# Another order and other engines for the operations between a convolution and a mix, and other banks for the last projections

## The chip, the cores and the metric

The kernel runs on one core of a Trainium2 chip. The metric is the device time of a run in microseconds; the time of a kernel is the median of its runs. Profiles are of one execution each, and give the span from the first instruction to the last.

## The reference, cut to what matters

```python
# A: 2048 tokens, 640 channels, bf16
h = _layernorm(A_q) * (1 + ca) + sa                # ca, sa, ga, sb, cb, gb from silu(c) @ w_mod
kv = short_conv(A_k, A_shift_k) * A_v              # 4 taps
y = irfft(rfft(kv, 2S) * rfft(ssm_k, 2S))[:S] + kv * ssm_D   # long convolution over the sequence
x = A_q + ga * (h * y)
# B: gated MLP whose gate mixes tokens
h = _layernorm(x) * (1 + cb) + sb
z = gelu(h @ B_w_in)                               # 640 -> 1728
z1 = z[..., :864]
z2 = _layernorm(z[..., 864:])
g = einsum('ts,bsf->btf', B_w_sp, z2) + b_sp       # 2048 x 2048 over tokens
out = x + gb * ((z1 * g) @ B_w_out)                # 864 -> 640
```

## The kernel before, in words

The long convolution is done as matrix products with cosine tables, in five blocks of 128 channels (u = 0 to 4). Its result multiplies gh (the normalised, modulated q) and is added to xt, the residual stream in bf16: these are the residual adds (`res`, L698), with the statistics of the second layernorm behind them (`ln2`, L704).

Then come 16 token tiles of 128, in four groups of four (`z_group`). For one group:

- aggregates of the statistics (`ag2`, L829), 1/sqrt on POOL (`rstd2`, L190 and L191), a small product (`nmr2`, L833);
- the norm of each tile into a tile of the tag Z (`zx`, L843 on ACT, L845 on POOL, L847 on VectorE);
- a transposition: group 0 by TensorE in two halves (`hfl`, L858), groups 1 to 3 by one DMA transpose on SP's queue (`turn`, L889), into another Z tile; the tag Z has three buffers;
- the modulation by cb and sb (`hmod`, L869 and L871, in group 0; `hmod2`, L895 and L897, in the others), five instructions for a group;
- 16 z products of five matmuls each (`zz`; all of TensorE's helpers stand on L245), eight for z2 and eight for z1, each into one bank of the tags pu or pz (two banks each), which GELU on ACT empties (L920);
- for z2 its own layernorm: bn_stats (`stz`, L926), aggregate (`agz`, L930), `rstdz` on POOL, `nmrz` (L935) and the norm in place (`zn`, L941 on ACT, L943 on VectorE). z1 is laid over tables that are no longer read (M2 and G2).

The mix is a product of 2048 x 2048 weights with z2, done in pairs of token tiles p and p + 8 with seven products of eight matmuls in place of eight (a Strassen-like scheme). It needs sums of weights (S, `s_sum`, L988), differences of z2 (T, `t_sum`, L998: T1, T2, T4, and one in place in z2) and seven products per pair (`product`, L1013). VectorE adds the products and multiplies by z1 (c11, partial, c22, last_sum) into u, a DMA transpose turns u into uT (`turn_u`, L1052), and `project` multiplies uT by w_o (L1137), adds xt (L1139) and stores. The w_o rows are multiplied by gb once they are in (`gbm`, L1077). The weights' tiles wT come by DMA transposes (`load_w`, L974), two per pair.

Everything up to and with the first pair of the mix (p = 0) is recorded as numbered operations, and `ORDER` lists in which order they are emitted and on which engine: P is TensorE, A ScalarE (ACT), D VectorE (DVE), G GpSimd (POOL), S SyncE (SP). The order is written out; each engine's queue is its subsequence, in order, and waits by semaphores. `FILLS` are operations of a few matmuls whose results nobody reads (numbers 1032 to 1037). Pairs 1 to 7 and the projections follow as a plain loop.

For reading the order: group 0's norms are 762, 763, 775, 776; group 1's are 840 to 843, its transpose 844 and its modulation 845 to 849; group 2's 906 to 909, 910 and 911 to 915; group 3's 972 to 975, 976 and 977 to 981. The rstdz of the groups are 828, 894, 960, 1026. The first pair's products are 1070, 1072, 1074, 1076, 1077, 1081, 1083; the T differences 1062 to 1069; the S sums of pairs 0 and 1 are 1054 to 1061; gbm is 1046 to 1052; w_o's loads are 1045; wT's loads 1038 to 1043.

Of the kernel before, what the change touches and what calls it, by code (L numbers as in the profile page):

```python
# [12 lines left out]
F32 = mybir.dt.float32  # L13
I32 = mybir.dt.int32

P = 128
# [50 lines left out]
G675 G519 G520 P521 A522 G509 G510 A500 A132 G708 P487 P584 D502 P513 D488 P511 A512 P491 P489 G503 A490 D514 P515  # L67
G504 D492 S678 G668 P505 P679 A516 A506 G493 D494 P495 A585 D633 D680 P681 D682 A496 P719 A720 D636 S586 P683 D684
P715 P721 A722 D716 P685 D686 D687 P717 A718 P587 A588 P723 P726 P725 G711 P724 G666 D688 D689 G714 D727 D728 D730
D729 D759 P735 P749 P589 A590 D758 D731 D732 G692 D690 G760 D761 D691 A762 G763 P1036 P1037 P764 D736 G611 D734 D750  # L70
D772 D733 D771 D766 S756 D767 D768 P765 A769 D751 P742 S757 A770 P814 G773 D774 G776 A775 D637 D712 D752 D737 D738
D741 P816 A817 G667 D739 P778 A782 D696 A783 D694 D835 D740 P784 D695 D836 P777 D779 D780 D781 G669 D837 D693 D834
D743 G702 G838 A815 D839 D840 D843 G841 A785 D610 D641 D643 D744 D745 P818 G697 D701 D699 A819 D698 P787 A788 D789
D786 P826 A827 A842 S844 P812 P794 A795 D796 D704 A813 G644 S1041 P798 S1045 P808 D642 D746 D901 A799 P820 G845 P824
D790 A809 A821 P801 A825 A847 P805 D703 D848 A802 P791 D849 D645 G846 P822 D810 A806 D807 P886 D705 P853 A792 A823
A887 D748 P882 D966 A883 D755 D903 P850 A854 D640 D900 D647 D793 P884 D700 D646 A851 D747 D902 A885 D754 G904 D905
D906 D909 S1040 G908 A907 S910 G913 D753 P864 S1038 A865 D866 D800 P890 A891 D706 D811 P892 A893 P871 A872 S1039 G911
D648 D969 P857 P860 A858 D859 A861 D803 D1048 P874 A875 D876 P880 A881 P878 P867 D968 A868 G912 P888 A889 D804 A879
G914 D915 P916 A917 D1058 P954 A955 P926 A927 D967 G970 P919 D971 D972 S1043 G975 D862 P923 D1051 A924 P937 G973 A920
D974 S976 A938 D863 P944 A945 D1054 D1055 D869 D870 D1050 D873 D1059 D1061 D1057 P958 A959 D925 S1044 P930 A931 D797  # L80
D877 A977 P933 D980 A934 P946 A947 G828 D829 D928 A831 A832 D833 P952 A953 D939 G978 P940 D1046 A941 G981 G979 P948
P999 A949 D932 P982 A1000 D852 D929 D855 D856 G894 A830 A983 D1053 P985 A986 D918 P1006 A1007 D935 P992 A993 D895 A896
D897 D942 D899 D898 P1012 D987 D1056 P989 A990 D994 P996 A997 D1008 D936 P1014 A1015 D943 D1049 D921 D922 P1003 A1013
P1020 D991 A1004 D1063 D1001 P1018 G960 D961 A963 A1021 A1019 D984 D988 D1005 D998 D1002 S1042 D1009 D995 G1026 D1062
P950 A951 P956 D964 D1027 D1028 D962 D965 D1064 A1029 D1030 A1031 D1065 D1066 D1067 P1024 A1025 P1070 A1071 A957 P1016
A1017 P1072 A1073 D1068 D1069 P1077 D1078 P1081 P1074 P1076 D1082 P1083 D1075 D1079 P1010 S1080 D1084 P1022 A1023
D1052 A1011 S1085 D1060 D1047
"""


# [39 lines left out]
def kernel(  # L130
# [80 lines left out]
    with ExitStack() as pctx:  # L211
# [745 lines left out]
        HT = NT // 2  # L957
        wTs, uTs, Ss, part, us, T = {}, {}, {}, {}, [], {}
# [20 lines left out]
        def a_of(p, i, j):  # L979
            return wTs[p + HT * i][:, j * HT:(j + 1) * HT, :]  # L980

        def s_sum(p, k):
            if k == 0:
                Ss[p] = [bwork.tile([P, HT, P], BF16, tag="S%d" % i, bufs=2, name="S%d" % (i + 1)) for i in range(4)]
            S = Ss[p]
            x, y, o = ((a_of(p, 1, 0), a_of(p, 1, 1), ALU.add), (S[0][:], a_of(p, 0, 0), ALU.subtract),
                       (a_of(p, 0, 0), a_of(p, 1, 0), ALU.subtract), (a_of(p, 0, 1), S[1][:], ALU.subtract))[k]
            nc.vector.tensor_tensor(S[k][:], x, y, op=o)  # L988
# [99 lines left out]
        for p in range(2):  # L1088
            for k in range(4):
                late("D", "ssum1" if (p, k) == (1, 0) else "ssum", lambda p=p, k=k: s_sum(p, k), r=[("wT", p), ("wT", p + HT), ("S", (p, {1: 0, 3: 1}.get(k, k)))], w=[("S", (p, k))])  # L1090
        for k in (1, 2, 3, 4):
            for h in range(2):
                lo, hi, name = h, h + 2, "T%d" % k
# [31 lines left out]
    psB = ctx.enter_context(tc.tile_pool(name="psB", bufs=2, space=bass.MemoryType.PSUM, reuse_waits="tile"))  # L1125
# [2 lines left out]
    def bank(b):  # L1128
        return psB.tile([P, 512], F32, tag="mm", bufs=6, name="ps")

    def project(t):
        ot = bwork.tile([P, D], BF16, tag="ot", bufs=3, name="ot")
        last = t == NT - 1
        for i, (lo, hi) in enumerate(((0, HS), (HS, HS + HS // 2), (HS + HS // 2, D)) if last else ((0, HS), (HS, D))):
            ps = psB.tile([P, 512], F32, tag="o", bufs=2, name="po")
            for ft in range(NFT):
                nc.tensor.matmul(ps[:, :hi - lo], lhsT=uTs[t][:fsz[ft], ft, :], rhs=w_o[:fsz[ft], ft, lo:hi],  # L1137
                                 start=(ft == 0), stop=(ft == NFT - 1))
            nc.vector.tensor_tensor(ot[:, lo:hi], ps[:, :hi - lo], xt[:, t, lo:hi], op=ALU.add)  # L1139
            if last:  # L1140
                (nc.scalar if i == 1 else nc.sync).dma_start(out_nat[:, t, lo:hi], ot[:, lo:hi])
        if not last:
            nc.sync.dma_start(out_nat[:, t, :], ot[:])
# [3 lines left out]
    for p in range(1, HT):  # L1147
# [5 lines left out]
        if nxt:  # L1153
            s_sum(p + 1, 0)
            s_sum(p + 1, 1)
# [11 lines left out]
        if nxt:  # L1167
            project(p - 1)
# [6 lines left out]
        if nxt:  # L1175
            project(p - 1 + HT)
            s_sum(p + 1, 3)
    for p in range(HT - 2, HT):
        project(p)
        project(p + HT)  # L1180


# [28 lines left out]
```

## Time and profile before

| | |
|---|---|
| time before, median of 3 runs | 314.79 us (314.57 to 317.16) |
| profiled execution | 315.2 us, its span 313.4 us |
| TensorE (PE) busy | 297.4 us, 2506 matmuls |
| VectorE (DVE) busy | 252.9 us, 513 instructions |
| ScalarE (ACT) busy | 159.9 us, 286 instructions |
| GpSimd (POOL) busy | 122.7 us, 152 instructions |
| granted TensorE clock | 1.00 |

The stretch from about 128 us to 207.6 us holds the four groups and the first pair of the mix, the stretch to 302 us the other seven pairs, and the rest is the last four projections. In a timeline a row gives the start, the time from the first to the last instruction of the row, the engine and line, output and inputs by their tile names (M, X and G stand for tiles that later hold z1 or z2), and in brackets how long the engine was idle before and who ended it.

### The profile page before, as it was taken

To read this page: it belongs to the slowest core of one execution; us is meant where nothing else is said; L and a number is where in the kernel's file an instruction comes from. 1 tells how busy PE (TensorE), PEld (TensorE's weight loads), DVE (VectorE), ACT (ScalarE), POOL (GpSimd) and SP (SyncE) were. 2 spreads that over 40 slices of the span, in tenths; PEclk is the share of its full clock that TensorE was granted. 3 is DMA by queue.
4 is the path that set the end of the run, shared out by engine and by line. 5 is a ranking of instruction groups with operands and counts; after the bars stand their busy time and mean duration, and the time that the engine had idled before them with its cause. 6 is when DMAs were issued, how large, how long until landed. Compare 5 with 4: busy or idle time off the path is not lost.

```text
span 313.4 us, 6409 instructions
## 1 busy us (share of the span) xinstructions
PE 297.4 (95%) x2506; PEld 196.9 (63%) x2506; DVE 252.9 (81%) x513; ACT 159.9 (51%) x286; POOL 122.7 (39%) x152
## 2 busy tenths in 40 slices
PE   7988999979999998999899999899999999999996
PEld 2665688857889998654454454455565656555554
DVE  7898998979999998989776898987676858567473
ACT  6988799968888957465655775320101010010100
POOL 2532877838988998675435524000000000000000
PEclk9999999999999999999999999999999999999999
DMA  8999899996997769206987700035958385540413
GB/s 163 216 229 239 225 315 250 216 183 165 246 198 145 164 126 323 81 0 138 225 168 156 111 2 1 1 74 120 200 78 192 66 171 118 119 100 4 99 38 104
DMA packets 127953, 45.22 MB, mean 144 GB/s; under 512 B 117071, under 2 KB 127156, under 8 KB 127924
## 3 DMA queue, kind: packets, MB, share of 16 engines
q1 hardware_dynamic: 127770, 44.78, 66.1%
q8 instruction: 19, 0.31, 0.4%
q14 instruction: 10, 0.08, 0.1%
q10 hardware_dynamic: 154, 0.05, 0.1%
HBM read 16.11 MB, written 5.24 MB: 68 GB/s over the span
## 4 chain that ended last, share of the span: by engine, by line
PE 38%; DVE 10%; POOL 5%; DMA 2%; ACT 1%; issue 1%; POOLq 0%; DVEq 0%; ACTq 0%
PE ps L1013 22%; PE po L1137 9%; DVE stz L926 3%; PE pu L245 3%; PE pz L1013 2%; DMA Z<-Z 2%; PE pz L245 2%; DVE S L988 1%; POOL rstdz L191 1%; POOL Z L897 1%; PE pu L1013 1%; DVE st L704 1%; POOL Z L845 1%; ACT X L941 1%; POOL rstd L191 1%
## 5 line engine op out<-in xcount | busy, mean ns | idle before, releaser
L245 PEld LDWEIGHTS <-Z 128*128 128x128 bf16 x320 | 30.7, 98 | 31.2 <-POOL Z L897 4.3
L245 PE MATMUL pu<-X,M 128*128 128x128 bf16 (+1 forms) x480 | 45.8, 237 | 2.2 <-DVE Tf L462 1.9
L245 PEld LDWEIGHTS <-M 128*128 128x128 bf16 x480 | 37.4, 98 | 8.6 <-issue 3.1
L1019 ACT COPY m<-ps 128x432 f32<-128x432 f32 x7 | 3.6, 519 | 72.3 <-PE ps L1013 72.3
L1013 PEld LDWEIGHTS <-S 128*128 128x128 bf16 x256 | 25.0, 98 | 23.6 <-issue 2.0
L476 POOL TENSOR_TENSOR W<-Tf 128x256 bf16<-128x256 f32 x47 | 34.7, 760 | 10.8 <-DVE Tf L462 7.5
L245 PE MATMUL pu<-big,Z 128*128 128x432 bf16 x160 | 33.1, 346 | 1.7 <-ACT X L920 1.3
L245 PE MATMUL pz<-big,Z 128*128 128x432 bf16 x160 | 33.5, 346 | 0.8 <-POOL Z L897 0.8
L248 ACT CAST X<-s 128x1024 bf16<-128x1024 f32 x31 | 31.9, 1028 | 2.9 <-PE s L245 2.7
L1137 PE MATMUL po<-w_o,uT 128*128 128x320 bf16 (+2 forms) x231 | 33.0, 295 | 0.4 <-DVE ot L1139 0.3
L462 DVE TENSOR_TENSOR Tf<-pu,KH 128x1024 f32<-128x1024 f32 x25 | 30.3, 1218 | 2.4 <-PE pu L245 1.3
L1137 PEld LDWEIGHTS <-uT 128*128 128x128 bf16 (+1 forms) x231 | 22.2, 98 | 10.3 <-issue 0.7
L1013 PEld LDWEIGHTS <-wT 128*128 128x128 bf16 x192 | 18.7, 98 | 15.2
L245 PEld LDWEIGHTS <-G 128*128 128x128 bf16 x330 | 24.7, 98 | 2.1 <-issue 0.2
L248 ACT CAST KH<-pu 128x512 bf16<-128x512 f32 x40 | 23.0, 600 | 5.1 <-PE pu L245 5.1
L248 ACT CAST Z<-pz 128x512 bf16<-128x512 f32 x38 | 22.3, 601 | 5.3 <-PE pz L245 5.1
L1013 PE MATMUL ps<-X,wT 128*128 128x432 bf16 x112 | 22.7, 346 | 0.0
L1013 PE MATMUL ps<-T,S 128*128 128x432 bf16 x112 | 22.7, 346 | 0.0
L245 PEld LDWEIGHTS <-X 128*128 128x128 bf16 x288 | 17.7, 97 | 7.7 <-DMA X<-kv_scr 2.4
L1013 PE MATMUL ps<-X,S 128*128 128x432 bf16 x112 | 21.6, 346 | 0.0
L245 PE MATMUL s<-F1bd,X 128*128 128x256 bf16 x128 | 19.2, 272 | 2.0 <-DVE X L400 1.6
L245 PE MATMUL sm<-big,dg 128*128 128x512 bf16 (+1 forms) x80 | 20.4, 379 | 0.0
(181 smaller groups left out, 546.6 us busy)
## 6 DMA issues: line engine op xcount, KB each, us to landing
wm<-in_w_mod_dram SPq DMA_DIRECT2D x6, 800.0 KB, 6.2
xt<-in_A_q_dram SPq DMA_DIRECT2D x4, 640.0 KB, 6.4
out_dram<-ot SPq DMA_DIRECT2D x15, 160.0 KB, 2.1
big<-in_B_w_in_dram SPq DMA_DIRECT2D x2, 1080.0 KB, 9.4
X<-in_A_ssm_k_dram SPq DMA_DIRECT2D x4, 512.0 KB, 5.3
kv_scr<-big SPq DMA_DIRECT2D x4, 512.0 KB, 4.1
X<-kv_scr SPq DMA_DIRECT2D x4, 512.0 KB, 4.9
w_o<-in_B_w_out_dram SPq DMA_DIRECT2D x6, 160.0 KB, 3.1
```

What stands on the lines that cost most here:

```text
L191: nc.gpsimd.tensor_tensor(dst, dst, mhalf[:, 0:dst.shape[1]], op=ALU.pow)
L245: nc.tensor.matmul(o, lhsT=w, rhs=x, start=start, stop=stop)
L248: (e.copy if e is nc.scalar else e.tensor_copy)(dst, src)
L462: e.tensor_tensor(T_[:], (tl[pu] if src is None else tl[src])[:, :, :, None, :].to_broadcast(shape), tl[KH][:, :, None, :, :].to_broadcast ...
L476: e.tensor_tensor(tl[W][:, :, o, :], T_[:, :, 0, o, :], T_[:, :, 1, 1 - o, :], op=ALU.add if o else ALU.subtract)
L704: op("D", "ln2", lambda e, n=n: e.bn_stats(out=st2[:, n, (0, 0, 0, 1, 2)[u], :], in_=xt[:, n, us[0] * DU:(u + 1) * DU]), r=[("xt", (v, n)) ...
L845: e.tensor_scalar(dst, xt[:, n, :], rstd2[:, n:n + 1], nmr2[:, n:n + 1], op0=ALU.mult, op1=ALU.add)
L897: e.tensor_scalar(h, h, cb1_col[:, dt:dt + 1], sb_col[:, dt:dt + 1], op0=ALU.mult, op1=ALU.add)
L926: op("D", "stz", lambda e, i=i, n=n, fc=fc: e.bn_stats(out=stz[:, n, fc, :], in_=tl[z2][:, i, fc * FC:(fc + 1) * FC]), r=[(z2, (i, fc))], ...
L1013: nc.tensor.matmul(ps[:, :FC], lhsT=lhs[:, s_, :], rhs=rhs(s_), start=(s_ == 0 and not more), stop=(s_ == HT - 1), skip_group_check=more)
L1019: nc.scalar.copy(part[p, m][:], part[p, BANK[m]][:, :FC])
L1137: nc.tensor.matmul(ps[:, :hi - lo], lhsT=uTs[t][:fsz[ft], ft, :], rhs=w_o[:fsz[ft], ft, lo:hi], start=(ft == 0), stop=(ft == NFT - 1))
```

## The change: what it does

The last 18 rows of `ORDER` are replaced, `s_sum` allocates its four tiles at whichever of its calls comes first, and the last four calls of `project` take their banks from the tag mm (six banks, used by the mix's products until then) and not from o (two banks). All operations, their shapes and their number stay.

```diff
-D729 D759 P735 P749 P589 A590 D758 D731 D732 G692 D690 G760 D761 D691 A762 G763 P1036 P1037 P764 D736 G611 D734 D750
+D729 D759 G702 D729 P735 P749 G667 D758 D731 P1037 P589 A590 D732 D734 D691 D772 G760 D761 D762 D763 P764 D750 P765 D766
...
         def s_sum(p, k):
-            if k == 0:
+            if p not in Ss:
                 Ss[p] = [bwork.tile([P, HT, P], BF16, tag="S%d" % i, bufs=2, name="S%d" % (i + 1)) for i in range(4)]
...
-    def project(t):
+    def project(t, tag="o"):
...
-            ps = psB.tile([P, 512], F32, tag="o", bufs=2, name="po")
+            ps = psB.tile([P, 512], F32, tag=tag, bufs={"o": 2, "mm": 6}[tag], name="po")
...
     for p in range(HT - 2, HT):
-        project(p)
-        project(p + HT)
+        project(p, "mm")
+        project(p + HT, "mm")
```

The queues that the two orders give, by operation number, from the norms of group 0 on; first TensorE's:

```
before 589 1036 1037 764 765 742 814 816 778 784 777 818 787 826 812 794 798 808 820 824 801 805 791 822
       886 853 882 850 884 864 890 892 871 857 860 874 880 878 867 888
       916 954 926 919 923 937 944 958 930 933 946 952 940 948
       999 982 985 1006 992 1012 989 996 1014 1003 1020 1018 950 956 1024 1070 1016
       1072 1077 1081 1074 1076 1083 1010 1022
after  1037 589 764 765 742 784 816 812 794 777 778 787 818 824 820 814 805 791 822 808 801 826 798
       850 860 864 884 892 867 857 890 880 888 878 871 874 886 853 882
       926 916 948 952 923 946 919 954 933 940 958 930 944 937
       999 982 992 1020 989 985 1006 996 1003 1024 1014 956 1016 1012 950
       1072 1070 1077 1081 1074 1076 1083 1010 1018 1022 1036
```

SP's:

```
before 844 1041 1045 1040 910 1038 1039 1043 976 1044 1042 1080 1085
after  844 1045 1041 1040 910 1038 1044 1039 976 1042 1043 1080 1085
```

POOL's:

```
before 711 666 714 692 760 763 611 773 776 667 669 702 838 841 697 644 845 846 904 908 913 911 912 914
       970 975 973 828 978 981 979 894 960 1026
after  711 666 714 702 667 760 692 773 775 838 841 644 610 669 846 904 908 911 970 973 975 974 828 980
       894 978 981 960 1026
```

Norms, modulations and norms of z2 that change their engine:

| operations | before | after |
|---|---|---|
| 762, 763 (norms, group 0) | ACT, POOL | VectorE |
| 775, 776 | ACT, POOL | POOL, ACT |
| 842 (norm, group 1) | ACT | VectorE |
| 845, 847 (modulation, group 1) | POOL, ACT | VectorE |
| 848, 849 | VectorE | VectorE, ACT |
| 907 (norm, group 2) | ACT | VectorE |
| 912, 913, 914 (modulation, group 2) | POOL | ACT, ACT, VectorE |
| 972, 974 (norms, group 3) | VectorE | ACT, POOL |
| 979, 980 (modulation, group 3) | POOL, VectorE | ACT, POOL |
| 611, 697, 610 (residual adds) | POOL, POOL, VectorE | VectorE, VectorE, POOL |
| zn on VectorE | 9 of 16 | 12 of 16 |

The fill of four (1036) stands before the flips of group 0 (764) in the old order and after the last z product of the recorded part (1022) in the new one. The S sums of pair 1 stand partly behind the first pair's products in the old order (1060) and all before them in the new one; gbm the other way round (six of seven behind them).

More of the change, by code (lines that the diff above doesn't have):

```diff
@@ L69 @@
 P715 P721 A722 D716 P685 D686 D687 P717 A718 P587 A588 P723 P726 P725 G711 P724 G666 D688 D689 G714 D727 D728 D730
-D729 D759 P735 P749 P589 A590 D758 D731 D732 G692 D690 G760 D761 D691 A762 G763 P1036 P1037 P764 D736 G611 D734 D750
-D772 D733 D771 D766 S756 D767 D768 P765 A769 D751 P742 S757 A770 P814 G773 D774 G776 A775 D637 D712 D752 D737 D738
-D741 P816 A817 G667 D739 P778 A782 D696 A783 D694 D835 D740 P784 D695 D836 P777 D779 D780 D781 G669 D837 D693 D834
-D743 G702 G838 A815 D839 D840 D843 G841 A785 D610 D641 D643 D744 D745 P818 G697 D701 D699 A819 D698 P787 A788 D789
@@ L74 @@
[L74 to L87, printed above, removed]
+D759 G702 D729 P735 P749 G667 D758 D731 P1037 P589 A590 D732 D734 D691 D772 G760 D761 D762 D763 P764 D750 P765 D766
@@ new lines @@
+D767 D768 D733 D690 D771 P742 S756 G692 D696 D736 D737 D739 D740 A769 A770 S757 P784 A785 G773 D774 P816 A817 A776
+P812 D637 D695 D836 G775 A813 P794 A795 D693 D741 D738 D834 D837 D694 D835 P777 D779 D780 D781 P778 A782 G838 D839
+D840 D843 A783 P787 A788 D842 G841 D751 S844 D754 D697 D712 D743 D611 D700 D744 D748 G644 P818 P824 A825 D701 A819
+D699 D746 P820 A821 P814 P805 A806 G610 D641 P791 D642 G669 D643 S1045 A815 D796 S1041 P822 A792 A823 D640 D747 D902
+D848 D845 D847 P808 A809 D901 G846 P801 A849 A802 D745 D698 D706 D900 P826 D648 P798 A799 P850 D903 A851 D852 P860
@@ new lines @@
+A827 A861 P864 A865 P884 A885 P892 D1050 G904 D905 P867 A868 D906 D907 D909 A893 P857 P890 A858 A891 S1040 P880 A881
+D793 P888 A889 G908 D803 S910 D755 P878 A879 P871 D645 G911 A913 A872 S1038 P874 P886 D866 D800 A875 P853 P882 A912
+A887 A854 D705 A883 D869 D647 D968 D752 D704 D810 D753 D646 D967 D969 D703 D966 D1060 D914 D1058 G970 D971 D915 A972
+G973 D859 D804 P926 P916 A917 D1059 G975 D807 A927 D811 D789 P948 D876 S1044 D1053 P952 S1039 D1056 D928 D873 D877
+A949 P923 A924 G974 D870 P946 A947 A953 D855 P919 A920 D786 D790 D925 D797 P954 D1054 A955 D862 D863 G828 P933 A934
@@ new lines @@
+S976 G980 P940 A979 A941 P958 A977 P930 A931 D856 G894 D1061 A959 D929 D1055 D1057 D942 D935 P944 A945 P937 D918 A938
+D895 D898 A899 D897 D896 G978 D921 D922 D829 D832 G981 D939 D943 P999 D932 D936 G960 P982 A1000 D830 A983 D984 S1042
+D1001 P992 A993 P1020 A1021 D961 P989 A990 D1063 D833 P985 A986 P1006 A1007 A962 P996 A997 D965 P1003 A1004 D831 P1024
+D994 D991 D995 D987 D988 P1014 D1008 P956 D1005 D1009 A1025 A1015 P1016 D998 D1002 G1026 D963 D1062 A964 D1064 D1027
+D1030 A957 A1017 P1012 A1013 S1043 P950 A1029 A951 P1072 A1073 D1028 P1070 D1031 D1065 A1071 D1066 D1067 P1077 P1081
@@ L88 @@
+D1068 D1069 D1078 D1082 P1074 P1076 P1083 D1075 D1079 S1080 P1010 A1011 D1084 D1048 P1018 A1019 P1022 A1023 D1049
+D1052 S1085 D1051 P1036 D1047 D1046
 """
```

## The prediction

> **What bounds the kernel now.** I read the busy shares first, then the waits of TensorE, then its timeline at each wait, and last a table of stages.
>
> ```profile
> PE 297.4 (95%) x2506; PEld 196.9 (63%) x2506; DVE 252.9 (81%) x513; ACT 159.9 (51%) x286; POOL 122.7 (39%) x152
> ```
>
> TensorE is the bound and the change gives it no matmul more or fewer, so the time can only move by what TensorE waits. Its waits from 150 us on (us in total, times, longest), then its timeline around them (start, us, idle before in brackets):
>
> ```profile
> PE pz L1013 <- ACT G L920: 1.8, 1, 1.8
> PE pu L245 <- ACT X L920: 1.3, 1, 1.3
> PE pz L245 <- POOL Z L897: 0.8, 1, 0.8
> PE pu L245 <- POOL Z L897: 0.4, 2, 0.2
> PE po L1137 <- DVE ot L1139: 0.3, 1, 0.3
> ```
>
> ```profile
> 128.87 1.89 PE L245 MATMUL s<-ident 128*128 128x512 bf16 x7
> ...
> 132.37 1.36 PE L245 MATMUL pz<-big,Z 128*128 128x432 bf16 x5
> ...
> 147.41 1.08 PE L245 MATMUL pz<-big,Z 128*128 128x432 bf16 x5
> 149.79 1.17 PE L245 MATMUL pu<-big,Z 128*128 128x432 bf16 x5 [1.30 <-ACT X L920]
> ...
> 178.12 0.53 PE L245 MATMUL pz<-big,Z 128*128 128x432 bf16 x2
> 179.40 0.72 PE L245 MATMUL pz<-big,Z 128*128 128x432 bf16 x3 [0.75 <-POOL Z L897]
> 179.96 1.08 PE L245 MATMUL pu<-big,Z 128*128 128x432 bf16 x5
> ...
> 194.20 1.08 PE L245 MATMUL pz<-big,Z 128*128 128x432 bf16 x5
> 197.02 1.62 PE L1013 MATMUL pz<-T,S 128*128 128x432 bf16 x8 [1.75 <-ACT G L920]
> ```
>
> The reader is to see that each wait is one late hand-over at the head of a token group, and that the fills at 128.87 stand in a wait too. From 207.80 the mix has none:
>
> ```profile
> 207.80:302.06 94.26, 94.26 (x560) 54.61 (x559) 63.90 (x113) 8.94 (x16) 0.00 (x0) 1.00 0.53 111
> ```
>
> So whatever reaches the mix's second pair earlier ends earlier by as much. A z product (five matmuls) lasts 0.913 (150.79 to 151.70), a mix product 1.46 (197.02 to 198.48).
>
> [...] the trace keeps clock 1.00 over the 1.75 us wait, so moving fills away should cost no clock. [...] an S sum (L988) took 1.08 at 169.11 beside GpSimd's norms, 0.67 alone. This is the unknown in every VectorE sum below.
>
> **The change part by part.** I walk the new per-engine queues by hand from the common point at 128 us, with durations of the timelines: norm of xn2 0.40 on VectorE, 1.10 on POOL, 0.92 on ACT; modulation 0.36, 0.92, 0.81; bn_stats 0.52 (432), 0.33 (256), 0.20 (128); aggregate 0.14; zn 0.41 on VectorE, 1.05 on ACT; S sum 0.65; T difference 0.97; GELU 0.43; rstd pair 1.3. For each hand-over I compare when it is ready with when TensorE asks.
>
> *Head of group 0.* Now ACT and POOL normalise tiles 0 and 1 (129.71 to 130.72) and the flips start at 130.81. Both norms move to VectorE: free at 129.75 after three short statistics, plus 0.80, so flips at 130.65. Modulation then follows one 0.60 product on VectorE and starts at 131.2, not 131.91. The first z product starts at 132.1 unbroken, where today's five at 132.37 take 1.36. Tiles 2 and 3 are ready for flipping at 135.9; four z products end at 135.75. Six are done at 138.4 against 139.19: gain 0.8.
>
> *Group 1.* Its rstd waits for aggregates that end at 136.9 (139.3 now); the norms go to VectorE (three) and POOL, end at 139.7, not 142.18, and the transpose is issued 2.4 earlier. It lands 5.3 to 5.8 later, at 145.5 at most. VectorE has 6.35 us queued after its norms (four residual adds, a gh add, a y product, twelve statistics, an aggregate), reaches the modulation at 145.95 and ends its three at 147.05. TensorE asks at 138.4 + 10 x 0.913 = 147.55. Cover 0.5; gain 149.79 - 148.32 = 1.47.
>
> *SP's queue.* The seven w_o loads move ahead of the first wT load. They wait for the last residual add on POOL (139.7 plus three adds of 1.2, 143.3), so SP stands there, and both wT loads and the second transpose stand behind: 3.9 + 2 x 3.1 gives 153.4 for a transpose whose data are ready at 151.6. It lands at 158.7, its modulation ends at 161.5 (VectorE's last waits behind nmr, that behind POOL's rstd at 161.0). TensorE asks at 147.55 + 16 x 0.913 = 162.2. The 1.8 that SP's order costs lies in that slack; gain 166.13 - 164.48 - 0.91 = 0.74.
>
> *Group 3.* xn2's tile shares three Z buffers, so its norms can't start before group 1's last product (162.2). POOL does three, to 165.6; the transpose lands at 171.0; POOL modulates three with an rstd between: 175.1. TensorE asks for the first at 175.0 (ACT's, ready 173.2) and the last at 175.7. Cover 0.6; gain 0.93, and 0.14 of a small gap at 176.3.
>
> *First pair of the mix.* Today's 1.75 is a bank: GELU of G stands on ACT behind zn, which stands behind nmrz and POOL's rstdz (192.05 to 194.15). In the new order all z2 halves of group 3 end by 184.2 with six z1 halves after them, rstdz ends at 186.4, T1 at 186.4; the bank is free at 188.2, and TensorE arrives at 188.7. T2 needs ACT's zn at 189.3, so 190.35 against 191.65; the differences in place (L998) 192.3 against 193.1; T4 194.2 against 197.5. Gain 1.91. S sums of pair 1 come before the products and gbm after them; pair 0's project asks for w_o nine us later, so neither costs.
>
> *Fill of four* (op 1036): from the wait at 128.87 to after the last z1 half, where TensorE waits for nothing: [...] Bounds 0 (if a wait stands there) and 1.0 (four sevenths of 1.89).
>
> *Projections in mix banks.* Today the third projection bank waits for VectorE's add behind the last products of u (304.39), and the last piece again. With six banks the four project at 302.06 + 56 x 0.1365 = 309.7 plus 0.17 of drain, against 310.57: gain 0.7. Below that it isn't limited: the last uT lands near 306.9 and is asked for at 307.8. Bounds 0.3 (the wait row) and 0.8.
>
> *More on VectorE*: seven instructions (two norms, a modulation, three zn, a residual), 2.8 us, all in the sums above.
>
> **Sum.** 0.8 + 1.47 + 0.74 + 0.93 + 0.14 + 1.91 - 0.9 + 0.7 = 5.8 us if each cover holds. The covers of 0.4 to 0.8 are as large as the spread of a transpose (0.5) and smaller than 2% of 60 us of VectorE (1.2), so I take 0.8 of new waits: 5.0. The profiled execution took 315.2 (span 313.4 and 1.8 around); 310.2 for it. The median, 314.79, is 0.4 below, so 309.8.
>
> **The rivals.**
> - *Half is given back* in transposes: VectorE is locked out near 140 and SP comes late, so groups 1 and 3 wait about 1.2 each and the mix 0.5 more. For it: covers of 0.5 and 0.6. Against: SP has 3.5 us of slack at the second. 314.79 - 5.8 + 2.9 = 311.9.
> - *Each wait only moves* to the next hand-over: VectorE is 81% busy, and a TensorE that arrives early finds it late. Then the tail's 0.7 and the head's 0.8 remain, less the fill: 314.2.
> - *VectorE becomes the bound, slower than before.* Place: its queue from group 2's modulation to the last T difference (161 to 194), where my walk leaves it about 1 us idle. Price: a meeting with one of POOL's 11 instructions there costs 0.4 (1.08 less 0.67) up to that instruction's whole length, about 1. It decides from 5.8 + 0.8 us of lateness, which is 0.6 at each of the 11. At 0.8 each it is 8.8 late, 8.0 of it on the path: 314.79 - 5.8 + 8.0 = 317.0. Against it: the trace shows the larger of these prices nowhere.
> - The projection's banks could be ones still read; the two first come from the pair before and are long free, so I give that nothing.
>
> **How the numbers follow.** Forecast 309.8 with chance 0.62 (its own range 308.6 to 311.3), half given back 0.18, only moved 0.11, VectorE bound 0.09. The range runs from 308.0 to 314.3, which leaves out the slower case and a little at each end. By over 1% (3.1 us, about what can be told from no change), below 311.6: the forecast and half of the second: 0.73; within 1%: 0.17; slower: 0.10.
>
> **What would show it.** Right: TensorE at the mix's second pair near 203 instead of 207.6; no wait over 0.6 between 147 and 200; transposes issued near 140, 153 and 166; four fills as a block before that pair; projections at the end with no wait for VectorE. Wrong: a wait of TensorE on L998's T or X, on Z modulated by VectorE, or VectorE without a gap from 161 to 194 with TensorE waiting for it.

## The result and the profile after

The changed kernel takes 313.75 us (median of 20 runs, 312.76 to 315.13), the kernel before 314.85 beside it; the ratio is 0.9968, interval 0.9949 to 0.9986. That is a gain of about 1.0 us, where 5.0 were forecast. Its profiled execution took 314.39 us, its span 312.6.

TensorE's waits from 124 us on (engine, tile and line, whom it waits for: us in total, times, longest):

```profile
PE s L858 <- DVE Z L847: 2.2, 1, 2.2
PE pu L245 <- DVE Z L897: 2.1, 1, 2.1
```

and its timeline there and at the end of the recorded part:

```profile
130.47 1.07 PE L858 MATMUL s<-ident,Z 128*128 128x128 bf16 x6 [2.20 <-DVE Z L847]
...
150.66 1.68 PE L245 MATMUL pu<-big,Z 128*128 128x432 bf16 x5 [2.06 <-DVE Z L897]
152.13 2.01 PE L245 MATMUL pz<-big,Z 128*128 128x432 bf16 x5
153.93 1.32 PE L245 MATMUL pu<-big,Z 128*128 128x432 bf16 x5
155.09 1.08 PE L245 MATMUL pz<-big,Z 128*128 128x432 bf16 x5
...
206.37 1.03 PE L245 MATMUL s<-ident 128*128 128x512 bf16 x4
207.45 1.62 PE L1013 MATMUL ps<-X,wT 128*128 128x432 bf16 x8
```

None of the waits listed for the kernel before is left, and two longer ones stand at the heads of groups 0 and 1, both ended by VectorE. From 151 us on the list has no wait of TensorE. The three products behind the second wait are slow: 150.66 to 155.09 is 4.43 us where three of 0.913 take 2.74. The profile's clock row says the same:

```profile
PEclk9999999999999999899799999999999999999999
```

The trace's clock records have a granted clock of 0.5 there in two spells of 3.41 us each, from 130.53 and from 151.01; I call such a spell a halving.

The profiled executions do not start alike: the first transposition at L721 lies between 121.05 and 124.28 us in those of this document, though the order up to there is the same. So I cut the span at four places of TensorE: the first transposition at L721 (122.61 before, 121.20 after), group 1's first z product (op 850 after, 886 before), the first product of pair 1, and the first of the last projections.

| stretch, us | before | after |
|---|---|---|
| A: L721 to group 1's first z product | 27.17 | 29.46 |
| B: from there to the mix's second pair | 57.82 | 56.80 |
| C: mix to the last projections | 94.46 | 94.46 |
| D: from there to the last instruction of an engine | 8.85 | 8.19 |

A has lost 2.29 although it was to gain. B has gained 1.02 in spite of the fill, 1.03 in it, and of 1.69 of slow products (4.43 less 2.74): without both it is 3.74 shorter. D gains 0.66; the last store's 2.5 us stand behind it in both. In sum the profiled execution of the changed kernel takes 0.6 longer from L721 on than that of the kernel before, and ends earlier only because its L721 came 1.41 earlier; the median of 20 runs is the measure of the gain. A stage of one execution is not exact either: the kernel with the tail alone (below) has the old order up to the mix, and its B is 58.53 and not 57.82.

Why A is late is seen in VectorE's and then GpSimd's rows, first at the head of group 0, then at group 1:

```profile
125.82 0.90 DVE L698 TENSOR_TENSOR xt<-xt,gh 128x256 bf16<-128x256 bf16 x1
...
129.19 0.87 DVE L833 SCALAR_TENSOR_TENSOR nmr<-mv,rstd 128x2 f32<-128x2 f32 x1
...
139.41 1.56 DVE L847 TENSOR_SCALAR Z<-xt,mv,rstd 128x640 bf16<-128x640 bf16 x3
140.89 1.36 DVE L698 TENSOR_TENSOR xt<-xt,gh 128x512 bf16<-128x512 bf16 x1
...
142.50 1.05 DVE L698 TENSOR_TENSOR xt<-xt,gh 128x512 bf16<-128x512 bf16 x1
143.47 1.37 DVE L661 TENSOR_TENSOR gh<-gh,gsa_bf 128x512 bf16<-128x512 bf16 x1
...
149.93 0.99 DVE L897 TENSOR_SCALAR Z<-Z,cb_col,sb_col 128x512 bf16<-128x512 bf16 x3
```

```profile
124.06 2.51 POOL L698 TENSOR_TENSOR xt<-xt,gh 128x512 bf16<-128x512 bf16 x2 [0.85 <-DVE gh L678]
...
128.90 1.14 POOL L698 TENSOR_TENSOR xt<-xt,gh 128x512 bf16<-128x512 bf16 x1
...
140.76 3.80 POOL L698 TENSOR_TENSOR xt<-xt,gh 128x512 bf16<-128x512 bf16 x3
```

Each of those VectorE instructions, the norms at 139.41 and the modulation at 149.93 apart, takes two to six times what it takes alone (0.29, 0.16, 0.41, 0.41, 0.41), and each lies beside a residual add that GpSimd had started before it. They last about as long as the rest of that add, which I call the lock: the one of 129.19 ends at 130.06, GpSimd's at 130.04; the last ends at 144.84, GpSimd's three at 144.56. In the kernel before, GpSimd's run of three adds lies for the most part beside statistics (its row is the second):

```profile
134.91 0.68 DVE L704 BATCH_NORM_STATS2 st<-xt 128x6 f32<-128x128 bf16 x3
```

```profile
134.57 3.54 POOL L698 TENSOR_TENSOR xt<-xt,gh 128x512 bf16<-128x512 bf16 x3
```

and three statistics take 0.68 there. In these rows the instructions that take longer, at L698, L661 and L833, have two inputs in SBUF; the statistics have one, and the product L746, whose second input is in PSUM, takes 0.42 at 125.36 beside GpSimd's pair of adds, as it does in the kernel before (0.42 at 126.78). The new order moved VectorE's two-input instructions beside GpSimd's adds; the old one had mostly statistics there. It was not free of the lock, though, and its profile showed the price before the change:

```profile
141.51 0.94 DVE L698 TENSOR_TENSOR xt<-xt,gh 128x512 bf16<-128x512 bf16 x1
```

That add lies beside a norm of GpSimd (141.13 to 142.17). Two more, at 134.14 and 143.15, took 0.73 and 0.59 and not 0.41; the three lost 1.03 us, the five of the new order lose 3.87. Two things are less simple. The three norms at 139.41 have one tensor input each, and yet the third, beside GpSimd's norm (139.75 to 140.79), takes 0.84 where the first two take 0.45 and 0.44; why is not shown. And a gh add (L661) at 133.61 in the kernel before took its 0.41 although a norm of GpSimd had begun at 133.46, so not every meeting locks.

### The profile page after: what moved, and what is told of

Same layout as the page of the kernel before. It is cut to its first block, busy times and chain, and to the rows that moved or that the text cites. A ratio compares the mean times of both kernels' runs of the same rounds, so it can differ in the third digit from the quotient of the medians.

```text
span 312.6 us, 6393 instructions
## 1 busy us (share of the span) xinstructions
PE 298.4 (95%) x2499; PEld 198.7 (64%) x2506; DVE 259.9 (83%) x520; ACT 158.0 (51%) x284; POOL 117.8 (38%) x147
## 4 chain that ended last, share of the span: by engine, by line
PE 51%; DVE 6%; POOL 0%; issue 0%
PE ps L1013 23%; PE po L1137 10%; PE pu L245 7%; PE pz L245 7%; DVE st L704 2%; PE pz L1013 2%; PE pu L1013 1%; DVE xt L698 1%; DVE Z L847 1%; DVE gh L746 1%; DVE gh L661 0%; DVE mv L829 0%; DVE Z L871 0%; POOL rstd L191 0%; PE s L245 0%
## 5 line engine op out<-in xcount | busy, mean ns | idle before, releaser
L245 PEld LDWEIGHTS <-Z 128*128 128x128 bf16 x320 | 31.8, 100 | 30.7 <-DVE Z L897 2.7
L245 PE MATMUL pz<-big,Z 128*128 128x432 bf16 x160 | 32.7, 353 | 0.0
L245 PE MATMUL sm<-big,dg 128*128 128x512 bf16 (+3 forms) x73 | 20.0, 382 | 0.4
```

The costliest lines, as they stand in the source:

```text
L245: nc.tensor.matmul(o, lhsT=w, rhs=x, start=start, stop=stop)
```

## The experiments

Theory: A is late because GpSimd's adds lock VectorE out. Rivals: the queue ahead of the modulation is too long in itself; a TensorE that loses its fills runs at a halved clock, and this is what costs; a wait only moves to the next hand-over. Edits are to the changed kernel unless told otherwise. "Under before" is (1 - ratio) x 315 us. Each ratio is against the kernel before as timed beside that run. Its interval is 0.5 to 1.4 us on each side, so two kernels less than about 1 us apart are not told apart by their times, and there only the profiles speak, of one execution each. The halved clock is read from the mean clock of each run: half of 3.41 us is 0.0055 of 312.6, so I take about 0.995 as one halving and 0.989, which the profiled execution with its two has, as two. That is an estimate from this one trace.

**One edit at a time.** The fill back at the head:

```diff
-D761 D762 D763 P764
+D761 D762 D763 P1036 P764
...
-D1051 P1036 D1047
+D1051 D1047
```

> The changed kernel, with the fill of four matmuls (1036) back in front of the flips of group 0. Clock theory (2.2 us of idleness before the flips at 130.5 halve the clock for the next 3.41 us): the wait shrinks by the fill's 0.9 to 1.3, the clock stays whole at that place, the first six z products are done 1.1 us earlier, and the 1.0 us of the fill at the end goes: 2.1 us less than the changed kernel, 311.7; the wait at group 1 grows by the 1.1, if VectorE's queue sets it, and then only 1.0 of it is kept: 312.7. Rival (the halvings come with the load of the chip, not with a wait): the halving near 130 stays, and the fill's 1.0 alone is kept.

Measured: 0.9946 (0.9924 to 0.9968), 1.7 under before. A is 29.20, only 0.26 less; the fill's 1.03 is gone from B; group 1's wait is 2.5, with a halved clock behind it.

Group 1's modulation early:

```diff
-D744 D748 G644
+D744 D848 D845 D847 D748 G644
...
-D902 D848 D845 D847 P808
+D902 P808
```

> The changed kernel, with VectorE's three modulations of group 1 (848, 845, 847) moved in front of ten statistics, behind the residual add 744. Theory (TensorE waits for VectorE's queue, and the 2.1 us of it halve the clock for 3.41 us): the transpose has landed at 146.8, the three end at 148.0 before TensorE asks at 148.4, both the wait (2.1) and the slow z products (1.7) go: 3.8 us less than the changed kernel, 310.0. Rival (the transpose or SP's order is what is late): the wait stays above 1.5 and the time within 0.7 of 313.75. Rival (VectorE is full, and what it does first is paid later): the same wait comes back at group 2 or at the first pair of the mix.

Measured: 0.9987 (0.9966 to 1.0008), no gain over the changed kernel. The wait at group 1 is gone and A falls to 27.48, but B rises to 57.12 (the changed kernel's 56.80 held 1.69 of slow products, this one holds none): TensorE now waits 0.5 for ACT at 164 and 0.6 for GpSimd at 179. In this form the wait moved, and I had not expected it.

GpSimd's three adds on VectorE:

```diff
-D751 S844
+D751 D644 D610 D669 S844
...
-D748 G644 P818
+D748 P818
...
-G610 D641
+D641
...
-G669 D643
+D643
```

> The changed kernel, with the three residual adds that POOL does from 140.8 to 144.6 (644, 610, 669) on VectorE, at the same place. VectorE has three instructions more and POOL three less. Lock theory (beside POOL's adds VectorE's took 1.36, 1.05 and 1.37 and not 0.42): six adds at 0.42 take 2.5 instead of 3.8, VectorE reaches group 1's modulation at 148.6 and not 149.9, the wait falls from 2.1 to 0.8, no halving there: 3.0 us less, 310.8. Work theory (VectorE simply has too much): 1.3 us later, 151.2, the wait grows to 3.4 and the time to 315.

Measured: 0.9932 (0.9911 to 0.9952), 2.1 under before. With three instructions more, VectorE starts the modulation at 149.20 and not 149.93, although L721 lies 0.9 later in that execution; group 1's wait is 0.35, A 27.78. That speaks for the lock and against a queue that is too long in itself.

The fill before group 1 instead of at the end:

```diff
-A799 P850
+A799 P1036 P850
...
-D1051 P1036 D1047
+D1051 D1047
```

> The changed kernel, with the fill of four (1036) in front of the first z product of group 1 (850). Clock theory: TensorE's wait there falls from 2.1 to 1.2, too short to halve the clock; the 1.7 us of slow z products go and the fill's 1.0 at the end too, though the wait itself ends at the same time: 2.7 us less, 311.1. Rival (the clock has nothing to do with the wait): the halving near 151 stays and 1.0 is gained, 312.7.

Measured: 0.9954 (0.9933 to 0.9975), 1.4 under before. Group 1's wait is 1.6, not the 1.2 expected, and the clock of the profiled execution is 1.00. Of the 21 runs compared, 14 have a clock of 0.999 or 1.0, and they are no faster (median 314.2) than the other seven (313.9). So these times do not show a cost of the halved clock.

**The head alone, and two fills.** Adds 667 and 692 on VectorE:

```diff
-P749 G667 D758
+P749 D758
...
-S756 G692 D696
+S756 D667 D692 D696
```

> The changed kernel with residual adds 667 and 692 on VectorE (just ahead of the statistics 696), nothing else. Theory (GpSimd's adds lock VectorE out at the head of group 0): the residual add before the statistics takes 0.4 and not 0.9, the small product nmr of the first two tiles 0.16 and not 0.87, so that the flips start 1.0 to 1.2 earlier and their wait falls from 2.2 to 1.1; no halved clock there. But TensorE then arrives earlier at group 1, where VectorE is as late as before: that wait grows from 2.1 to about 3, so the time is within 0.5 us of the changed kernel, 1 to 1.5 under the kernel before. Rival (the head is what costs, and group 1's wait is a consequence of the halved clock): 2.5 us under the kernel before.

Its VectorE rows and TensorE's waits:

```profile
125.67 0.29 DVE L698 TENSOR_TENSOR xt<-xt,gh 128x256 bf16<-128x256 bf16 x1
...
128.43 0.10 DVE L833 SCALAR_TENSOR_TENSOR nmr<-mv,rstd 128x2 f32<-128x2 f32 x1
```

```profile
PE pu L245 <- DVE Z L897: 2.5, 1, 2.5
PE s L858 <- POOL Z L845: 1.1, 1, 1.1
PE s L858 <- DVE Z L847: 0.8, 1, 0.8
```

Measured: 0.9969 (0.9948 to 0.9990), as the changed kernel. Both instructions are back at their own length and the first z product comes 9.56 us after L721 instead of 11.46. The wait at group 1 grows to 2.5, a new one of 1.1 stands at the second flips, and nothing is won: TensorE only comes earlier to a VectorE that is late.

Both waits with a fill in them (1036 before 764, 1037 before 850):

```diff
-D731 P1037 P589
+D731 P589
...
-D763 P764
+D763 P1036 P764
...
-A799 P850
+A799 P1037 P850
...
-D1051 P1036 D1047
+D1051 D1047
```

> The changed kernel with the fill of four (1036) back before the first flips (764) and the fill of three (1037) moved from before op 589 to before group 1's first z product (850): TensorE computes the same, and each of the two long waits has a fill in it. If the halved clock costs what the profiled execution shows (1.7 us each time): no halving in most runs, and 1.5 to 2 us under the changed kernel beyond the 0.9 of the fill, so 3.5 to 4 us under the kernel before. If the slower products are mostly absorbed by the next wait for VectorE, or seldom fall where they count: 2 us under the kernel before, like the kernel with the first fill alone moved back.

Measured: 0.9933 (0.9903 to 0.9963), 2.1 under before: the second of the two expectations. Five of the eight runs still have a halving (clock 0.993 to 0.995).

**All at once, then one taken back.** Fill 1036 at the head, five adds on VectorE, the modulation ahead of statistics (shown where each now stands; it is gone from its old place):

```diff
+S756 D667 D692 D696
...
+D763 P1036 P764
...
+D751 D644 D610 D669 S844
...
+A815 D848 D845 D847 D796
```

> The changed kernel with every suspected loss taken away at once: the fill of four (1036) back before the first flips (764); five residual adds (667, 692, 644, 610, 669) on VectorE in place of GpSimd; group 1's modulation on VectorE (848, 845, 847) before op 796, ahead of seven of the statistics that held it up. Theory (the forecast's gains are there, and were lost to VectorE being locked by GpSimd's residual adds and to the queue ahead of the modulation): flips about 1.2 earlier than in the kernel with the fill alone moved back, no wait over 1 us of TensorE at group 1's first z product (850), clock 1.00 in most runs, pair 1 of the mix 80 to 81 us after the first transposition of block 4 (85.2 in the kernel before, 84.9 with the fill alone moved back); time 4.5 to 5.5 us under the kernel before. Rival (a wait only moves: five adds more on VectorE come back as waits at groups 2, 3 or the first pair): a wait of 1 to 2 us of TensorE on VectorE between 160 and 195, time 2 to 2.5 us under the kernel before, as with three adds moved.

Measured: 0.9873 (0.9839 to 0.9908), 4.0 under before, 3 under the changed kernel; A 25.95, B 55.77, D 8.18. VectorE and TensorE's waits:

```profile
140.61 1.41 DVE L698 TENSOR_TENSOR xt<-xt,gh 128x512 bf16<-128x512 bf16 x4
...
142.47 0.41 DVE L661 TENSOR_TENSOR gh<-gh,gsa_bf 128x512 bf16<-128x512 bf16 x1
```

```profile
PE pz L245 <- POOL Z L897: 1.3, 2, 1.0
PE s L858 <- POOL Z L845: 1.1, 1, 1.1
```

Four residual adds take 1.41 where one took 1.36. The two waits on VectorE are gone, and two others of 2.4 in sum have come up; part of what is missing from the forecast may lie there.

From this kernel I took back one part at a time. First, 644, 610 and 669 on GpSimd again:

> The kernel with all losses taken away, but the three residual adds 644, 610 and 669 on GpSimd as in the changed kernel. Theory (GpSimd locks VectorE out for as long as its adds run): VectorE's two residual adds and its gh product at 140 to 145 take 1.0 to 1.4 instead of 0.4, its group 1 modulation starts about 1.5 later although it has three instructions fewer, TensorE waits 0.8 at op 850; 0.8 us slower than with all losses taken away. Rival (those durations are VectorE's own, and the gain of the earlier run came from elsewhere): three instructions of 0.42 fewer let the modulation start 1.2 earlier, no wait, no slower.

```profile
141.55 1.36 DVE L698 TENSOR_TENSOR xt<-xt,gh 128x512 bf16<-128x512 bf16 x1
...
143.16 1.05 DVE L698 TENSOR_TENSOR xt<-xt,gh 128x512 bf16<-128x512 bf16 x1
144.13 1.37 DVE L661 TENSOR_TENSOR gh<-gh,gsa_bf 128x512 bf16<-128x512 bf16 x1
```

Measured: 0.9951 (0.9929 to 0.9972), 1.5 under before: 2.5 us of the gain lost, three times what I had expected. The durations are the changed kernel's again, and op 850 waits 1.2 for VectorE. Group 2 waits another 0.9, by a longer way: the w_o loads on SP wait for VectorE's last residual add, so the second transposition behind them is issued 33.95 us after L721 and not 32.24, and it also landed later (6.8 us after its issue, where all in the kernel with everything taken away took 5.3 to 5.4). How the 2.5 divides between the two is not measured. The clock is at 0.999 or more in all 14 runs. Of the parts taken back, three adds on the wrong engine cost the most, and they cost it with no halved clock.

The modulation where the changed kernel has it:

> The kernel with all losses taken away, but group 1's modulation on VectorE where the changed kernel has it (behind 796, 640, 747 and 902). Theory: it starts at about 149.2 instead of 146.7 on that profile's clock, TensorE asks at 147.7 and waits 1.5 to 1.9 at op 850; 1.4 us slower. Rival (the wait is absorbed by those that come later, at group 3 and the first pair): under 0.5 slower.

Measured: 0.9846 (0.9810 to 0.9882), 4.8 under before, no slower. Its profile has a wait of 0.8 at op 850, less than my 1.5 to 1.9, and in exchange one of 0.3 instead of 1.3 at group 3 (B 54.60). The rival was right here: with the five adds on VectorE, no loss by the modulation's place is seen.

The fill at the end again:

> The kernel with all losses taken away, but the fill of four (1036) where the changed kernel has it, behind the last z product. Theory (the forecast's term): the flips start no earlier, since they wait for VectorE, and the four matmuls cost 1.0 in full at the end of the stretch: 0.9 to 1.0 us slower, the clock stays 1.00 since only 1.1 us of waiting is left at the head. Rival (without the fill the clock is halved at the head): a halved clock in most runs and 1.7 us more, so 2.6 slower.

Measured: 0.9892 (0.9859 to 0.9926), 3.4 under before, 0.6 to 1.4 less than the three kernels with all these adds moved that have it at the head. That is about the fill's 1.0, though the intervals of 1.1 to 1.4 on each side leave it open; no run has a halved clock. The profiled execution shows 1.9 more in B, the 1.03 of the fill and a wait of 1.0 for ACT in group 2: there a transposition landed 7.2 us after its issue.

Two edits more, in the kernel with all at once, for the two waits left there:

```diff
-S756 D667 D692 D696 D736
+S756 G773 D667 D692 D696 D774 D736
...
+D1061 D978
```

> The kernel with all losses taken away at once, and two edits more for the two waits that its profile still has: the small product nmr of tiles 2 and 3 (774) directly behind the statistics 696, for the second flips (1.1 us of waiting for GpSimd's norm), and modulation 978 of group 3 on VectorE behind the S sum 1061, not on GpSimd behind rstdz (1.0 and 0.3). Theory (what is left between 4 us and the forecast's 5 is these two waits): both waits under 0.3, pair 1 about 80.5 us after the first transposition of block 4 (81.7 without the edits), time 5 us under the kernel before, 1 us under the kernel without the edits. Rival (each wait only moves): the 1.1 comes back as a wait at group 1's first z product, which had 0.7 of cover, or at the first pair; no faster than without the edits.

Measured: 0.9861 (0.9817 to 0.9905), 4.4 under before. Both waits are gone; a new one of 0.9 on the modulation L871 of group 0 is there, and L721 to pair 1 is 80.89 against 81.73. In time it can't be told from the kernel without the two edits.

**The tail alone**, in the kernel before:

```diff
-        project(p)
-        project(p + HT)
+        project(p, "mm")
+        project(p + HT, "mm")
```

> The kernel before with only the last four projections in the tag mm. Theory: from the first of the last projections to the end 10.7 us and not 11.4, time 0.7 us under the kernel before. Rival (the wait was hidden or comes back as another, such as the store): no difference.

Measured: 0.9983 (0.9965 to 1.0000), 0.5 under before, at the edge of what can be told; D is 8.19 in place of 8.85, as in every kernel with the change.

**The clock.** Both waits filled to the brim, or left empty; these two kernels differ in nothing but matmuls that nobody reads (1036 stands before 764, 1037 before 850):

```diff
-FILLS = (4, 6, 2, 2, 4, 3, )
+FILLS = (4, 6, 2, 2, 12, 10, )
```

> The changed kernel with its two long waits of TensorE filled: fill 1036 before the first flips with 12 matmuls, fill 1037 before group 1's first z product with 10 (22 matmuls in place of 7, nobody reads them; all else is as in the changed kernel). Theory A (the halved clock is a cost of its own): no halved clock, and 1.5 us faster than the same kernel with one matmul in each fill, although TensorE computes 20 matmuls more. Theory B (VectorE sets the end of group 1, so slow products at the head are absorbed there, and slow products behind group 1 come in few runs): within 0.5 us of the other.

```diff
-FILLS = (4, 6, 2, 2, 4, 3, )
+FILLS = (4, 6, 2, 2, 1, 1, )
```

> The same with one matmul in each of the two fills, so that TensorE is idle for 2 us and more in both waits. Theory A: a halved clock in nearly every run, twice in many, 1.5 us slower than with the waits filled. Theory B: a halved clock in most runs, and the time within 0.5 us of the kernel with the waits filled. Both: 1.5 to 3 us under the kernel before.

TensorE's timeline with the waits filled, then with them empty:

```profile
148.60 2.32 PE L245 MATMUL s<-ident 128*128 128x512 bf16 x10
151.24 1.09 PE L245 MATMUL pu<-big,Z 128*128 128x432 bf16 x5 [0.32 <-DVE Z L897]
```

```profile
133.31 1.07 PE L858 MATMUL s<-ident,Z 128*128 128x128 bf16 x6 [2.63 <-DVE Z L847]
...
135.50 4.62 PE L245 MATMUL pu<-big,Z 128*128 128x432 bf16 x15
...
152.38 0.38 PE L245 MATMUL s<-ident 128*128 128x512 bf16 x1
152.76 1.09 PE L245 MATMUL pu<-big,Z 128*128 128x432 bf16 x5
```

Measured: filled 312.96 us, 0.9934 (0.9911 to 0.9957), clock 0.999 or more in all 18 runs; empty 312.90, 0.9935 (0.9916 to 0.9954), a halving in all 22 (0.995 or less), two in nine of them (0.989 or less). There is no difference; nor is there one among the empty one's runs (nine with two halvings 312.89, thirteen with one 312.92). The empty one shows why: 15 products take 4.62 and not 2.90, and group 1's wait has vanished. What the slow clock costs TensorE at the head, it would have waited for VectorE anyway. The intervals leave room for some 0.9 us, not for theory A's 1.5. The halving behind group 1, where nothing absorbs it, costs 1.69 on the changed kernel's trace; how often that falls in a run isn't known.

## Why the prediction was wrong

| term, us | forecast | measured |
|---|---|---|
| head of group 0 and group 1 (A) | -2.27 | +2.29 |
| groups 2 and 3, first pair (B without fill and slow products) | -3.72 | -3.74 |
| fill of four | +0.9 | +1.03 |
| last projections (D) | -0.7 | -0.66 |
| sum | -5.8 | -1.1 |

The sum of the measured terms is near the time that was won (1.0 by the ratio); the slow products of 1.69 in the profiled execution are left out of it, which is a choice, made because that execution is the only one of the 20 with two halvings (clock 0.989; the others have 0.993 to 0.995). Taken with them, it alone gives 0.6 in the other direction. The second line agrees to 0.02 by luck in part: B differs by 0.7 between two executions of the old order. The error stands in the first line, 4.56 us; the 0.8 that I held back for new waits was less than a fifth of it.

The step that failed is the walk of VectorE's queue ahead of the first z products of groups 0 and 1. Each instruction stood in it at the length that it has alone, and the lock, which I had called the unknown in every VectorE sum, stood in no sum. In its place the traces show 1.32 us of lock at the head and 2.55 at group 1.

- *Head of group 0*: wrong. Forecast: first z product 9.49 us after L721; measured 11.46. The lock makes the residual add 0.61 and the small product 0.71 longer, and the halved clock adds 0.6 (130.47 to 132.66 is 2.19, with the losses taken away 1.58), and 0.6 more in the three products behind (132.66 to 136.01). With the two adds moved it was 9.56.
- *Group 1*: VectorE's queue between norms and modulation was put at 6.35 us; it took 9.0 (140.9 to 149.93). Three locked instructions account for 2.55 (0.95 + 0.64 + 0.96), and 6.35 + 2.55 is 8.9. A cover of 0.5 stood against a price of 2.55. The queue also began late: the transposition was to be issued 2.4 us earlier than before, and was issued 19.86 us after L721, where the kernel before has 19.60. The wait on a Z tile modulated by VectorE, named ahead as a sign of being wrong, is the one of 2.06.
- *SP's queue and group 2*: the turns were issued at 141.06, 155.71 and 168.69, later than forecast, and no product waits for one; the slack was there. The w_o loads at 146.65 waited for VectorE's last residual add, which ends at 146.56, and not for GpSimd's, which end at 144.56. *Group 3* and the *first pair*: no wait, as forecast. Their gain is counted from a group 1 that is late, though. In the three kernels with all five adds moved, the modulation early or late, and the fill at the head, B was 54.6 to 55.8 and not 54.1: part of the later slack may have been TensorE's own lateness, though the difference is hardly larger than that of two executions.
- *Fill* and *tail*: right in the profiles (their own runs give 0.6 to 1.4 and 0.5 us, each within its interval of the forecast). The fill's 0.9 was an estimate; rows of three and of four such matmuls take 0.81 and 1.03 in the changed kernel, 0.22 a matmul, which gives 0.88 for four. *No cost for the clock*: wrong as a statement about the clock, since the one wait of 1.75 at clock 1.00 did not carry over to waits of 2.20 and 2.06; a cost in time was not found, with room for 0.9.
- *The rivals*: "each wait only moves" gave 314.2 and 0.11, and is nearest to what came; the kernel with the head alone mended shows it plainly. It is not the whole of it, since five adds moved at once, with the fill and the modulation, brought 3 us. The rival with VectorE as the bound named the right cause and price (0.61 to 0.96 us for one, in the changed kernel) and the wrong place: 161 to 194, where the changed kernel has no wait, and not 125 to 146. I had seen 1.08 for a locked S sum, and had overlooked the 0.94 at 141.51 for an add of 0.41, a loss of 0.53 and more than the 0.4 that I took as the lower price; and I had not asked which of VectorE's instructions would come to lie beside GpSimd's adds in the new order.

The version with all losses taken away beats both kernels by 4.0 and 3 us, with the modulation left in its place as much or more (4.8). Of the 6.0 forecast ahead of the mix, 4.1 (84.99 less 80.89) is the most that any profile here showed; which waits hold the rest is not settled.

## What to carry to other kernels

When an order moves work between VectorE and GpSimd, lay the two queues side by side and look in the profile for instructions of VectorE that take longer beside GpSimd's than alone. In the changed kernel five with two inputs in SBUF, each begun while GpSimd was at a residual add, took 0.61 to 0.96 us longer, until about the end of that add (a norm with one tensor input took 0.4 longer beside a norm of GpSimd). An add that frees VectorE of 0.41 us and costs it up to 0.96 is no relief. A cover of 0.5 was less than one such loss, and mending the head alone won nothing here until group 1, late on the same engine, was mended too.

## What the runs showed of the hardware that I had not expected

- A product of 128 x 2 values took 0.87 instead of 0.16, and ended at 130.06, beside a GpSimd add of 1.14 that ended at 130.04: the price of the lock went here by the other engine's instruction and not by the product's own 0.16.
- The granted clock was 0.5 for 3.41 us from 130.53 and again from 151.01, in each case within 0.4 us of the end of a wait (of 2.20 and of 2.06 us). The length of the wait did not settle it: a wait of 1.75 in the kernel before, waits of 2.2 and 1.6 in the kernel with the fill before group 1, and of 2.0 and 1.8 in the one with both waits filled lie in profiled executions with a clock of 1.00. What decides it was not shown.
- A halved clock was no loss of time that these runs can tell where a wait behind it absorbed it: 20 matmuls more or fewer, and a halving in none of 18 runs or in all of 22, gave 312.96 and 312.90, with room for 0.9.
